# Attention and feed-forward in one kernel: later loads for batch 2, wider runs for w_in, later token softmax, two more products by a second level of Strassen, and the states' first product by Strassen

## The chip, the cores and the metric

One NeuronCore of a Trainium2 chip runs the whole program. The metric is the device time of one execution in microseconds. A profile shows one execution, and its span runs from the first to the last instruction.

The engines are named as the profile names them: PE is TensorE (matmul), PEld its weight load, DVE is VectorE, ACT is ScalarE, POOL is GpSimd, SP is SyncE, which here only issues DMAs.

## The reference

There are 8 batches. In each, 512 tokens and 32 states exchange information by attention in 8 heads of 64 columns, and the 544 rows that result (8 heads side by side make 512 columns) pass through a feed-forward block with an ELU.

```python
# x (8, 8, 512, 64), state (8, 8, 32, 64): float32; w_in (512, 2048), w_out (2048, 512): float64
scores  = x @ state.T / 8              # per batch and head
xread   = softmax(scores) @ state      # 512 rows: tokens read states
scores2 = state @ x.T / 8
sread   = softmax(scores2) @ x         # 32 rows: states read tokens
r = concatenate([xread, sread])        # then (B*544, 512), heads side by side
h = r @ w_in
g = where(h > 0, h, exp(min(h, 0)) - 1)
out = g @ w_out
```

The result is float32, (4352, 512).

## The kernel before, in words

**One order for all.** The program is not written engine by engine. Every helper adds operations to a list (`Plan.add`), with engine, an assumed cost, the regions read and written, and for a PSUM tile a bank yet to be chosen. `Plan.order` then runs a list schedule: each engine takes, among the operations that are ready, the one with the earliest due time; PE takes them by their number in the list (`turn`). PSUM banks are handed out on the way; two of the eight (`fixed`) are kept for a special use, so six are free for the rest. What comes out is the instruction order of each queue. Until 40 us of assumed time, matmuls of the identity fill PE's gaps (`fill`). In the start the list's order is overruled by hand: `FIRST_PE` permutes PE's turns, `EARLIER` shifts due times, `FIRST_LOADS` ranks the first DMAs. As every record is made by one helper, nearly all have line L438 in the profile; they are told apart by tiles.

**The weights.** They arrive as float64 and are turned to float32 on the chip (`convert`: two ACT and four DVE operations for a block of 128 x 1024 values). There are 16 blocks of 1 MB: 0 to 7 from w_in, 8 to 15 from w_out. They pass through three raw buffers (`t_w`); a block's buffer is loaded again with the block three later once it is converted. w_out stays in SBUF. w_in goes through three slots (`w_half`), and is written to a DRAM tensor `w_in_mem` (`keep_w`), from which every later batch fetches it in eight pieces of 512 KB (`fetch`).

**Tokens.** As a head has only 32 states, the kernel does not form xread and multiply it by w_in: it forms m = state @ w_in per batch (`make_m`, small matmuls of 64 x 32 weights, in chunks `c` of 512 of the 2048 columns), and then h = softmax @ m. From batch 2 on this product is done by seven half-size products in place of eight (Strassen's scheme in Winograd's form, `ffn1_chunk`; the sums it needs are made by POOL, `sum_m` and `sum_a`). Batches 0 and 1, during which the weights arrive, use the plain product (`ffn1_plain`, one call per tile of 128 columns). `softmax` makes both softmaxes of a batch from one set of scores: the one over states (transposed, into `aT`) and the one over tokens (`soft_a`), which `move_state` or `turn_state` turn round for `state_read`.

**g @ w_out.** The class `Strassen` cuts g (512 x 2048) and w_out into quarters a11 to a22 and b11 to b22. The seven products are called here P1 = a11 b11, P2 = a12 b21, P3 and P4 with b22 and the sum t4, P5 with t1, P6 with t2 and P7 with t3 = b12; `sum_1` and `combine` make the sums of quarters of g on DVE. From batch 1 on, some of the seven are themselves done by seven products of 128 columns (class `Second`: `weights` makes the sums on the weight side once, `sums` those on the side of g, `steps` the seven products of four calls; after each, DVE or ACT takes the result out of PSUM and adds it into the output tile `o`). In `ffn2` of batches 2 to 7 these are P3 to P7; P1 and P2 are plain, sixteen calls of 256 columns each, in one PSUM bank. In batch 1 they are P3, P4, P5 and P7. Between P1 and P2 stand the scores and the first `make_m` of the next batch, and its softmax follows.

**States.** The 256 rows of sread of all batches come last (`states`): a plain first product in 64 calls of 256 columns, ELU, then one level of Strassen with w_out, and stores by quarters (`quarter`).

**The start** (`start`). States and x of batches 0 and 1 and the first weight blocks are loaded; for every block a `w_step` converts it, makes m for both batches, and the feed-forward of the two batches follows as chunks become ready. Batch 2's x is loaded a second time in a blocked form (`load_blocks`, sixteen DMAs of 64 KB in runs of 128 bytes) and turned round by DVE (`turn_blocks`) for its scores.

Of the kernel before, what the change touches and what calls it, by code (L numbers as in the profile page):

```python
# [21 lines left out]
ENGINES = (POOL, PE, DVE, ACT, SP)  # L22

# [58 lines left out]
class Plan:  # L82
# [99 lines left out]

    def prepare(self):
        for op in self.ops:
            op.users = []
            op.turn = self.places.get(op.number, op.number)
        for op in self.ops:
            for d in op.deps:
                d.users.append(op)
        self.opening = {}  # L190
        self.closing = {}
        for b in self.banks:
            self.opening.setdefault(b.first, []).append(b)
            self.closing.setdefault(b.last, []).append(b)
        self.kept = {b.first: b.fixed for b in self.fixed}
        self.all_banks = min([op.number for op in self.kept], default=0)
# [29 lines left out]
    def run(self, until=0.0):  # L226
# [4 lines left out]
        free_at[PE], free_at[ACT] = 0.7, 0.0  # L231
# [111 lines left out]
    def order(self, passes, until=0.0):  # L343
# [3 lines left out]
        for _ in range(passes):  # L347
# [8 lines left out]
            if best is None or last < best[0]:  # L356
                steps = [(op.start, op.number, op) for op in done]
# [4 lines left out]
        for at, n, op in steps:  # L362
            op.start = at
        return [op for _, _, op in steps], fills

@with_exitstack
def kernel(
# [36 lines left out]
    ).tile([P, 2 * FC, NP, 256], FP32, name="w_in_mem")  # L404
# [19 lines left out]
    w_half = buffer([3, NP, 256], "w_half")  # L424
# [94 lines left out]
    def dma(out, in_, tokens=((), ()), queue=SP, kind="dma"):  # L519
        size = 4 * elements(out) * out.shape[0]  # L520
        engine = nc.sync if queue == SP else nc.scalar
        op = plan.add(
            queue, 0.66 if kind in ("load_blocks", "move_state") else 0.44, issue(engine, "dma_start", dict(out=out, in_=in_)), [in_], [out],
            moved=size, tokens=tokens, name=kind,
        )
        if kind in ("load_x", "load_states", "load_blocks", "move_state"):
            op.rate = 230e3
# [108 lines left out]
    def fetch(hc):  # L636
        w = w_half[:, hc % 3]
        dma(w, w_in_mem[:, hc], tokens=((f"mem{hc}",), ()), kind="fetch")
        st["w", hc] = w

    def make_m(b, *hcs):
        c = hcs[0] // 2
        if hcs[0] % 2 == 0:
            st[b, "m", c] = [bank(), bank()]
        calls = []
        for hc in hcs:
            w, h = st["w", hc], hc % 2
            calls += by_state(
                b, st[b, "m", c], [w[:, m] for m in range(NP)],
                slice(h * 256, (h + 1) * 256), h == 0,  # L650
            )
        products(0.46 * len(hcs), calls, "make_m", "state")
# [4 lines left out]
    def copy_m(b, c, to, halves=False, engines=None):  # L657
        copies = engines or (A.copy, A.copy)
        for g in range(G):
            copies[g](out=to[:, g * 512 : (g + 1) * 512], in_=st[b, "m", c][g])  # L660
        g_of[b, c] = to

    def copy_m_half(b, hc, to):
        c, h = divmod(hc, 2)
# [31 lines left out]
    def soft_a(b, g):  # L696
        return (sec_2 if b < 2 else xr[:, 1024:])[:, g * 512 : (g + 1) * 512]
# [3 lines left out]

    def softmax(b, to):
        s = st[b, "s"]
        top, total = small[:, 0:2], small[:, 2:4]
# [5 lines left out]
        for g in range(G):  # L710
            V.transpose(out=soft_t(g), in_=s[g])
            V.reduce_max(out=tops(g)["top"], in_=s[g], axis=AX_X)
        V.tensor_scalar(out=top, in0=top, scalar1=-scale, scalar2=None, op0=ALU.mult)
        for g in range(G):
            A.activation(
                out=soft_a(b, g), in_=s[g], func=AF.Exp, scale=scale, bias=tops(g)["top"],
                accum_out=tops(g)["total"],
            )
# [13 lines left out]
        V.tensor_scalar(out=total, in0=total, scalar1=eps, scalar2=None, op0=ALU.add)  # L732
        V.reciprocal(out=total, in_=total)
# [61 lines left out]
    def ffn1_plain(b, c, g_to, a, e_slots):  # L795
        for q in range(4):
# [169 lines left out]
    }  # L966
    s_2 = [sec[:, 7680 + i * 1024 : 7680 + (i + 1) * 1024] for i in range(2)]
# [56 lines left out]
    def convert(dst, raw, pool_clamp=False, pool_add=False):  # L1024
# [3 lines left out]
        q = raw[:, : n // 2].rearrange("p n (j k) -> p (n j) k", j=2)  # L1028
# [4 lines left out]
        (Q if pool_clamp else V).tensor_scalar(  # L1033
# [10 lines left out]
        (Q if pool_add else V).tensor_tensor(out=bits, in0=bits, in1=q, op=ALU.add)  # L1044

    raws = [
        t_w_sb[:, i].rearrange("p k q -> p (k q)").bitcast(U32).rearrange("p (n k) -> p n k", n=4)
# [3 lines left out]
    def weight_block(n, parts=1):  # L1051

        out = []
        for i in range(parts):
            k = 4 // parts
            rows = slice(i * k, (i + 1) * k)
            raw = raws[n % 3][:, rows]
            if n < 8:
                src, dst = w_in_v[:, rows, n * 512 : (n + 1) * 512], w_half[:, n % 3, rows]
            else:  # L1060
                q, c = divmod(n - 8, 4)
                rows = slice(4 * c + i * k, 4 * c + (i + 1) * k)
                src = w_out_v[:, rows, q * 512 : (q + 1) * 512]
                dst = w_out[:, rows, q * 256 : (q + 1) * 256]
            dma(raw, src, kind="load_w")
            out.append((dst, raw))
        return out
# [3 lines left out]
    def ident_ready(i):  # L1071
# [12 lines left out]
    FIRST_PE = (  # L1084
        153, 48, 171, 198, 258, 106, 104, 86, 327, 32, 165, 16, 190, 265, 214, 157, 331, 90, 232,
        410, 335, 277, 261, 248, 169, 45, 289, 161, 202, 35, 146, 149, 347, 186, 210, 102, 339,
        173, 183, 408, 94, 229, 269, 218, 319, 194, 206, 98, 281, 113, 411, 293, 304, 414, 109,
        413, 409, 82, 351, 112, 273, 412, 38, 316, 307, 285, 42, 323, 79, 343,
    )
    FIRST_LOADS = (  # L1090
        6, 9, 0, 3, 5, 4, 1, 8, 7, 2, 12, 10, 11, 13, 14, 15,
    )
    EARLIER = {
        23: 34, 43: -2, 74: -5, 85: 22, 96: -17, 100: -12, 119: 28, 124: 25, 132: -3, 134: 2,
        135: 5, 136: 10, 137: 20, 138: -10, 142: 10, 154: -4, 163: 8, 175: 17, 195: 10, 199: 9,
        212: 10, 215: -2, 221: 10, 222: 10, 224: -15, 231: -10, 252: 2, 264: 10, 266: 10, 270: 20,
        272: 10, 276: 15, 280: 10, 282: -12, 283: 20, 286: -10, 288: -18, 295: 7, 306: 2, 311: 40,
        312: -10, 317: 5, 336: -2, 338: 12, 342: -2, 352: 7, 353: 42, 357: 10, 358: -2, 363: -12,
    }

    def start():
# [6 lines left out]
        m1.append(w_half[:, 2].rearrange("p m k -> p (m k)"))  # L1108
# [3 lines left out]
        blocks = {}  # L1112

        def read_block(n):
            blocks[n] = weight_block(n)

        def convert_block(n):
            for dst, raw in blocks[n]:
                convert(dst, raw)
            if n + 3 < 16:  # L1120
                read_block(n + 3)

        n = len(plan.ops)
        load_states(0, 1, raw_s, (SP, ACT))
        blocks[0] = weight_block(0, 2)
        load_x(0, x_halves, (SP, ACT))
        load_states(1, 2, raw_s[:, 1:], (SP,))
        read_block(1)
        load_x(1, x_1)
        read_block(2)  # L1130
        first = plan.ops[n:]
        for k, i in enumerate(FIRST_LOADS):
            first[i].rank = k
        turn_states(raw_s[:, 0:1], kT[:, 0:1])

        def w_step(hc):
            convert_block(hc)
            w = st["w", hc] = w_half[:, hc % 3]
            c = hc // 2
# [330 lines left out]
```

## Time and profile before

| | |
|---|---|
| time, median of 3 runs | 717.48 us (715.24, 717.48, 718.79) |
| profiled span | 715.3 us |
| PE clock granted | 0.998 |
| instructions | 13801 |
| DMA bytes | 78.49 MB, mean 110 GB/s |
| HBM read, written | 61.34 MB, 13.11 MB |

A busy line gives the time in which an engine works and the number of its instructions. A matmul call on float32 shows as two records. Matmuls are pipelined and the profile models their ends, so what one costs is read from start to start in the timeline, not from its duration. In a slice line each digit is the busy share in tenths of one of 40 equal slices (17.9 us each).

The profile's stages are: the start, up to about 113 us, while weights arrive; the rest of batches 0 and 1, up to about 200; batches 2 to 7, each 76.8 us apart; the states from 659.9 on.

### The profile page before, as it was taken

To read this page: it belongs to the slowest core of one execution; us is meant where nothing else is said; L and a number is where in the kernel's file an instruction comes from. 1 tells how busy PE (TensorE), PEld (TensorE's weight loads), DVE (VectorE), ACT (ScalarE), POOL (GpSimd) and SP (SyncE) were. 2 spreads that over 40 slices of the span, in tenths; PEclk is the share of its full clock that TensorE was granted. 3 is DMA by queue.
4 is the path that set the end of the run, shared out by engine and by line. 5 is a ranking of instruction groups with operands and counts; after the bars stand their busy time and mean duration, and the time that the engine had idled before them with its cause. 6 is when DMAs were issued, how large, how long until landed. Compare 5 with 4: busy or idle time off the path is not lost.

```text
span 715.3 us, 13801 instructions
## 1 busy us (share of the span) xinstructions
PE 700.3 (98%) x5526; PEld 588.3 (82%) x5526; DVE 525.5 (73%) x931; ACT 285.3 (40%) x547; POOL 122.7 (17%) x158
## 2 busy tenths in 40 slices
PE   8889999999999999999999999999999999999998
PEld 7434457888988899889988998889988998899886
DVE  3889899789549983899568964897489946976230
ACT  4978884011137311741075214631284017410320
POOL 0310000023211222220430241124212133000000
PEclk9999999999999999999999999999999999999999
DMA  9878770013163423541272316342444133001401
GB/s 243 258 172 316 251 265 26 1 25 121 63 165 84 116 53 107 157 118 30 94 202 63 86 62 148 105 120 73 122 115 121 29 118 119 0 1 40 150 21 27
DMA packets 133008, 78.49 MB, mean 110 GB/s; under 512 B 114000, under 2 KB 114512, under 8 KB 132944
## 3 DMA queue, kind: packets, MB, share of 16 engines
q1 hardware_dynamic: 130636, 76.99, 38.1%
q8 instruction: 43, 0.70, 0.4%
q10 hardware_dynamic: 2308, 0.62, 0.4%
q14 instruction: 21, 0.17, 0.1%
HBM read 61.34 MB, written 13.11 MB: 104 GB/s over the span
## 4 chain that ended last, share of the span: by engine, by line
PE 73%; DVE 14%; ACT 7%; DMA 4%; issue 1%; SPq 0%; DVEq 0%
PE ps L438 73%; DVE g L438 3%; DVE small L438 2%; DMA t_w<-in_moe_w_in_dram 2%; ACT sec L438 2%; DVE sec L438 2%; ACT xe L438 2%; DVE s L438 1%; DVE w_out L438 1%; DMA t_w<-in_moe_w_out_dram 1%; DVE xr L438 1%; DVE soft L438 1%; ACT w_half L438 1%; ACT t_w L438 1%; DVE t_w L438 1%
## 5 line engine op out<-in xcount | busy, mean ns | idle before, releaser
L438 PE MATMUL ps<-w_out,g 128*128 128x256 f32 (+1 forms) x960 | 174.7, 331 | 0.0
L438 PEld LDWEIGHTS ps<-w_out,g 128*128 128x128 f32 x960 | 151.1, 191 | 15.5 <-issue 2.5
L438 PE MATMUL ps<-aT,m 128*128 128x256 f32 (+1 forms) x568 | 149.2, 407 | 0.2 <-DVE g L438 0.2
L438 PEld LDWEIGHTS ps<-aT,m 128*128 128x128 f32 x568 | 105.4, 190 | 32.0 <-issue 12.2
L438 DVE TENSOR_TENSOR o<-o,ps 128x128 f32<-128x128 f32 (+2 forms) x214 | 60.4, 288 | 65.9 <-PE ps L438 64.0
L438 ACT ACTIVATE xe<-ps 128x512 f32<-128x512 f32 x104 | 58.9, 599 | 60.4 <-PE ps L438 47.8
L438 POOL TENSOR_TENSOR m<-m 128x256 f32<-128x256 f32 x72 | 51.5, 735 | 164.1 <-ACT m L438 162.7
L438 POOL TENSOR_TENSOR soft<-soft,small 128x512 f32<-128x512 f32 x32 | 33.8, 1075 | 234.8 <-DVE small L438 234.8
L438 PE MATMUL ps<-sec 128*128 128x128 f32 x544 | 72.6, 276 | 1.3 <-DVE o L438 1.3
L438 ACT COPY o<-ps 128x128 f32<-128x128 f32 (+2 forms) x55 | 21.9, 411 | 127.8 <-PE ps L438 126.0
L438 PE MATMUL ps<-t_w,s 128*128 128x128 f32 (+1 forms) x448 | 70.3, 306 | 0.0
L438 PEld LDWEIGHTS ps<-t_w,s 128*128 128x128 f32 x448 | 63.1, 191 | 6.5 <-issue 2.1
L438 PEld LDWEIGHTS ps<-sec 128*128 128x128 f32 x544 | 66.2, 192 | 2.2 <-DVE o L438 2.2
L438 ACT COPY m<-ps 128x512 f32<-128x512 f32 (+1 forms) x56 | 27.3, 529 | 79.0 <-PE ps L438 78.9
L438 DVE SCALAR_TENSOR_TENSOR g<-xe,ps 128x512 f32<-128x512 f32 x56 | 36.7, 680 | 26.7 <-ACT xe L438 23.9
L438 ACT COPY ps<-ps 128x512 f32<-128x512 f32 x24 | 13.7, 572 | 81.1 <-PE ps L438 81.1
L438 DVE TENSOR_TENSOR ps<-sec,ps 128x512 f32<-128x512 f32 x48 | 33.1, 690 | 10.8 <-PE ps L438 8.0
L438 PE MATMUL ps<-aT,s 128*128 128x256 f32 x168 | 40.2, 379 | 0.0
L438 PE MATMUL ps<-w_half,kT 64*32 64x256 f32 x1024 | 36.5, 385 | 0.2 <-DVE w_half L438 0.2
L438 PEld LDWEIGHTS ps<-aT,s 128*128 128x128 f32 x168 | 31.9, 190 | 4.3
L438 ACT COPY sec<-ps 128x512 f32<-128x512 f32 x48 | 28.3, 589 | 17.9 <-PE ps L438 17.9
L438 ACT ACTIVATE xe<-xe 128x512 f32<-128x512 f32 x56 | 33.4, 634 | 0.6
(112 smaller groups left out, 1012.1 us busy)
## 6 DMA issues: line engine op xcount, KB each, us to landing
w_half<-w_in_mem SPq DMA_DIRECT2D x56, 512.0 KB, 3.7
t_w<-in_moe_w_out_dram SPq DMA_DIRECT2D x8, 1024.0 KB, 6.5
t_w<-in_moe_w_in_dram SPq DMA_DIRECT2D x7, 1024.0 KB, 6.3
out_dram<-o SPq DMA_DIRECT2D x14, 512.0 KB, 2.7
xe<-in_x_dram SPq DMA_DIRECT2D x26, 256.0 KB, 2.9
o<-in_x_dram SPq DMA_DIRECT2D x80, 64.0 KB, 3.0
w_in_mem<-w_half SPq DMA_DIRECT2D x8, 512.0 KB, 6.8
xr<-xr SPq DMA_DIRECT2D x96, 32.0 KB, 1.9
```

The lines of the kernel that those rows point to most:

```text
L438: ins = getattr(engine, name)(**{k: resolve(v) for k, v in kw.items()})
```

## The change

It has seven parts.

- The first loads: x of batch 0 at the head of the queues, then the first two weight blocks. Batch 2's remaining state loads are put behind the conversion of block 9, and its blocked x behind that of block 15 (`plan.behind`).
- Blocks 0 to 7 of w_in are cut the other way: half the rows and 1024 words of columns (4 KB runs) in place of all rows and 512 words (2 KB runs). Blocks 0 and 1 are loaded and converted in halves (2 KB runs), so that half a chunk can be made from both; from then on a step takes a whole chunk, which is two blocks. `make_m` then makes 512 columns in one call where it made 256 in two.
- The token part of `softmax` becomes `softmax_rows`; in batches 0 and 1 it comes after chunk 1 of batch 0.
- The orders written by hand (`FIRST_PE`, `FIRST_LOADS`, `EARLIER`) go; the planner gets other assumed DMA rates (`DMA_COST`).
- P2 of batches 2 to 7 and P6 of batch 1 are done by `Second`.
- The states' first product is done by Strassen in four chunks (`state_chunk`), with five buffers for fetched pieces in place of three.
- The stores of the states are one DMA to a quarter in place of four, all on SP.

```diff
     w_in_mem = ...
-    ).tile([P, 2 * FC, NP, 256], FP32, name="w_in_mem")
+    ).tile([P, 2 * FC, 2, 512], FP32, name="w_in_mem")
-    def make_m(b, *hcs):
...
+    def make_m(b, c, part=None):
+        if not part:
             st[b, "m", c] = [bank(), bank()]
+        cols = slice(0, 512) if part is None else slice(part * 256, (part + 1) * 256)
+        products(
+            0.92 if part is None else 0.46,
+            by_state(
+                b, st[b, "m", c], [st["w", 2 * c + m // 2][:, m % 2, cols] for m in range(NP)],
+                cols, not part,
+            ),
+            "make_m", "state",
+        )
...
     def soft_a(b, g):
-        return (sec_2 if b < 2 else xr[:, 1024:])[:, g * 512 : (g + 1) * 512]
+        at = xr if b > 1 else s_buf if b else sec_2
+        return at[:, (b > 0) * 1024 + g * 512 :][:, :512]
...
+    second[2] = Second(sec_2)
...
+        if n < 8:
+            c, j = divmod(n, 2)
+            dst = w_half[:, n % 3]
+            src = w_in_v[:, 2 * j : 2 * j + 2, c * 1024 : (c + 1) * 1024]
...
     def start():
...
         load_states(0, 1, raw_s, (SP, ACT))
-        blocks[0] = weight_block(0, 2)
         load_x(0, x_halves, (SP, ACT))
+        read_half(0, 0)
+        read_half(1, 0)
         load_states(1, 2, raw_s[:, 1:], (SP,))
-        read_block(1)
         load_x(1, x_1)
+        read_half(0, 1)
+        read_half(1, 1)
         read_block(2)
...
         turn_x(x_halves, ob)
         scores(0, ob)
         softmax(0, a_sb)
-        w_step(1)
-        ffn1(0, 0)
-        turn_state(0)
+        w_half_step(0)
+        ffn1(0, 0, (0, 1))
         turn_x(x_1, ob)
         scores(1, ob)
-        state_read(0)
         softmax(1, aT1)
-        w_step(2)
-        ffn1(1, 0)
-        turn_state(1)
-        state_read(1, x_1)
-        w_step(3)
...
+        ffn1(1, 0, (0, 1))
+        w_half_step(1)
+        ffn1(0, 0, (2, 3))
+        ffn1(1, 0, (2, 3))
+        for c in range(1, 4):
+            w_step(c)
+            ffn1(0, c)
+            if c < 2:
+                for b in range(2):
+                    softmax_rows(b)
+                    turn_state(b)
+                    state_read(b, (x_halves, x_1)[b])
+            ffn1(1, c)
         for n in range(8, 16):
             convert_block(n)
+            if n == 9:
+                with plan.behind(plan.ops[-1]):
+                    load_states(2, B, raw_t, (SP,))
+                turn_states(raw_t, kT[:, 2:B])
+        late = plan.ops[-1]
...
-        load_blocks(2, xe)
+        with plan.behind(late):
+            load_blocks(2, xe)
...
     def ffn2(o, b, x1=None):
         if six:
...
             A.copy(out=c12, in_=x1)
+            A.copy(out=c11, in_=x1)
+            second[2].sums(o.a12, s_2[1], a_sb[:, :1024])
             if nxt:
                 scores(b + 1, xr)
                 first_m(b + 1)
-            o.product(x1, o.a12, b21, False)
-            A.copy(out=c11, in_=x1)
+            for f in second[2].steps(c11):
+                f()
...
         else:
+            A.copy(out=c12, in_=x1)
             combine(o.a12, o.a12, o.s)
+            second[6].weights(t_w[2])
+            second[6].sums(o.s, s_2[0], m_sb[:, 1, :1024])
             second[7].weights(t_w[3])
+            steps = second[6].steps(c12)
             second[7].sums(o.a21, s_2[1])
-            o.product(x1, o.s, t_w[2], False)
-            A.copy(out=c12, in_=x1)
-            A.copy(out=c21, in_=x1)
+            for f in steps:
+                f()
...
         if not six:
-            second[6].weights(t_w[2])
+            second[2].weights(b21)
...
+    def state_chunk(c, right):
...
+        V.tensor_tensor(out=s1, in0=l21, in1=l22, op=ALU.add)
+        V.tensor_tensor(out=s2, in0=s1, in1=l11, op=ALU.subtract)
+        V.tensor_tensor(out=l21, in0=l11, in1=l21, op=ALU.subtract)
+        V.tensor_tensor(out=s4, in0=l12, in1=s2, op=ALU.subtract)
...
+        product(pa, l11, r11, True)
+        A.copy(out=pb, in_=pa)
+        product(pc, s1, t1, True)
+        product(pb, s2, t2, False)
+        product(pa, l12, r21, False)
+        A.copy(out=u2, in_=pb)
+        elu(pa, to(0, 0), e_1, A)
+        product(pb, s3, t3, False)
+        A.copy(out=u3, in_=pb)
+        product(pb, l22, t4, False)
+        V.tensor_tensor(out=pa, in0=u3, in1=pc, op=ALU.add)
+        elu(pb, to(1, 0), e_2, A)
+        product(pc, s4, r22, False)
+        elu(pa, to(1, 1), e_1, A)
+        V.tensor_tensor(out=pc, in0=u2, in1=pc, op=ALU.add)
+        elu(pc, to(0, 1), e_2, A)
...
     o, x1 = start()
-    plan.places = dict(zip(FIRST_PE, sorted(FIRST_PE)))
-    for n, t in EARLIER.items():
-        plan.ops[n].nudge = t
```

## The prediction, made before the changed kernel ran

> **What bounds the kernel now.** First the engine shares, then the busy share by slice:
>
> ```profile
> PE 700.3 (98%) x5526; PEld 588.3 (82%) x5526; DVE 525.5 (73%) x931; ACT 285.3 (40%) x547; POOL 122.7 (17%) x158
> PE   8889999999999999999999999999999999999998
> DVE  3889899789549983899568964897489946976230
> ```
>
> TensorE is the bound, and from 113 us on nearly without a hole: the waits of PE in the window 113:715 list 2.5 us in all. So from there every us of matmul taken away shortens the span, unless a new wait takes its place. The chain of waits agrees: PE carries 73% of it. DVE is full only in places. Before 113 us it is another kernel; the windows by stage (PE, PEld, DVE, ACT, POOL busy, clock, DMA share, GB/s):
>
> ```profile
> 0.00:8.30 8.30, 6.94 (x39) 6.76 (x39) 0.00 (x0) 1.28 (x1) 0.70 (x6) 1.00 0.77 195
> 8.30:20.00 11.70, 10.09 (x146) 7.94 (x146) 8.88 (x18) 8.67 (x18) 2.05 (x2) 1.00 1.06 280
> 20.00:28.60 8.60, 7.33 (x138) 3.90 (x138) 7.63 (x15) 8.28 (x16) 2.91 (x2) 0.80 0.80 268
> 28.60:40.00 11.40, 10.24 (x76) 4.94 (x68) 10.49 (x21) 10.57 (x23) 4.15 (x4) 1.00 0.80 194
> 40.00:60.00 20.00, 18.13 (x155) 8.20 (x148) 16.01 (x22) 14.62 (x29) 0.00 (x0) 1.00 0.89 247
> 60.00:80.00 20.00, 18.75 (x88) 7.92 (x87) 17.42 (x23) 16.91 (x31) 0.00 (x0) 1.00 0.78 274
> 80.00:100.00 20.00, 19.78 (x114) 10.09 (x113) 19.50 (x26) 19.33 (x31) 0.00 (x0) 1.00 0.82 284
> 100.00:113.00 13.00, 11.48 (x39) 6.81 (x37) 13.00 (x18) 9.03 (x12) 0.00 (x0) 1.00 0.46 143
> ```
>
> PE's busy figure here includes fill matmuls. DVE, first used at 8.3, is busy 92.9 of the remaining 104.7 us; its holes (11.8 us) are mostly in 8 to 20 and 40 to 80. PE's first feed-forward matmul starts at 28.63; after that it is rarely dry for long. DMA is near its limit to 60 us. Three engines and the DMA share the bound, so no single relief gives much.
>
> Then the timeline of one steady second product (batch 3) and of the end:
>
> ```profile
> 313.81 1.09 PE L438 MATMUL ps<-xr,kT 64*32 64x512 f32 x16
> 314.69 1.07 PE L438 MATMUL ps<-w_half,kT 64*32 64x256 f32 x32
> 315.69 7.17 PE L438 MATMUL ps<-w_out,g 128*128 128x256 f32 x32
> 322.70 1.95 PE L438 MATMUL ps<-t_w,s 128*128 128x128 f32 x16
> 324.91 1.16 PE L438 MATMUL ps<-sec 128*128 128x128 f32 x8 [0.26 <-DVE o L438]
> ...
> 643.82 1.06 PE L438 MATMUL ps<-t_w,s 128*128 128x128 f32 x8
> 644.71 1.06 PE L438 MATMUL ps<-sec 128*128 128x128 f32 x8
> ...
> 659.90 27.79 PE L438 MATMUL ps<-xr,w_half 128*128 128x256 f32 x128
> 687.53 7.07 PE L438 MATMUL ps<-w_out,g 128*128 128x256 f32 x32
> ```
>
> Read starts, not durations: a plain P2 lasts from 315.69 to 322.70, 7.0 us, for 32 records (two to a call), about 0.216 each; a step of eight 128-column records takes 0.89 (643.82 to 644.71), 0.112 each; the states' first product 27.6. The small matmuls on 64x32 weights: 16 of 512 columns take 0.88 (scores), 32 of 256 take 1.00 (make_m; 1.02 at 341.24, where the next starts at 342.26).
>
> **What the skill says.** "TensorE: Matmul & The Clock Gate", section "Wait — 56ns, not 53.3ns?": warm matmuls start N / 2.4 GHz plus about 2.5 ns apart. That is 55.8 ns for 128 columns, and the trace's fp32 records show twice it, 112 ns, so the fixed part is there too: two records of 128 columns cost 0.224 where one of 256 costs 0.216, and seven products for eight save 9%, not 12.5%. "VectorE: DVE Perf Modes", "Mode 2×_2P": a tensor_tensor of fp32 cannot use the double rate; here 0.69 us for 512 elements against 0.44 for a TENSOR_SCALAR. "DMA: Bandwidth & Descriptors", "Specifications": under 512 B a descriptor is below line rate; the page counts 114000 such packets, and the slice with batch 2's 64 KB block loads shows 172 GB/s beside 251 and more around it.
>
> **The change, part by part.** The sum is made against the profiled span, 715.3.
>
> P2, batches 2 to 7. 7.0 becomes 7 x 0.89 = 6.25: -0.7 each, -4.2. Added on DVE per batch: four sums of 512 elements (4 x 0.69) and seven adds into o (0.28 each), 4.7 us; on ACT one copy more (0.58). P2 is just the work under which DVE now does softmax and the sums of P6: from 313 to 339 DVE has no hole over 0.3 us. But some 6.5 us of it is softmax (two transposes 0.71, maxima 1.25, four reductions of 0.67 or so, two xr transposes) which is wanted only by the batch after, about 8 us behind; from 340 to 356 DVE has 7 us of holes. So it can be put off, while s1 and s2 are wanted within the 1.8 us of the first two steps. PSUM is tight too: six banks for scores, m and two new ones. P6, of the same form in the same crowded place, loses 0.45 per batch (the gap at 324.9). I take +0.4 a batch, bounds 0 and 2.5 (a wait of 0.35 at each of seven steps): +2.4.
>
> P6 of batch 1: -0.7, but its weight sums (4 x 0.69) can only be written where batch 0's g lies, after the last product of batch 0; the first two steps cover 1.8 of it. +1.5 (0 to 4).
>
> make_m, batches 2 to 7: 24 calls with 512 columns in place of twice 256, the form of scores: 1.02 to 0.88, -0.14 x 24 = -3.4. Nothing is added; bounds -2.8 to -3.6. All steady fetches stay at 512 KB.
>
> States' first product: 128 x 0.216 = 27.6 becomes 224 x 0.112 = 25.0, -2.6. DVE per chunk of 6.25 us: four sums 2.76, two adds and four maxima at 0.42, together 5.3; ACT three copies and eight activations of 256 elements, 4.1. Both fit, and copies of one chunk lie under matmuls of the next. Before it, 1.7 (operand sums), 2.8 (chunk 0) and one more restore 0.7 must fit in the 0.6 us holes of DVE at 650 to 660. +0.4 (0 to 3).
>
> The start. Removed: from the SP queue, between weight blocks, 12 state loads (about 0.8 each) and 16 block loads (31.74 to 40.8 for nine, 42.0 to 49.9 for seven, 1 us each); the hand-written PE order and nudges; added: x of batch 0 at the head of both queues. Behind these loads on SP stood weight blocks, and ACT then waited 3.78 us for one at 47.1. x now lands by about 8 in place of 10.2 and scores(0) come 2 to 3 us earlier; the softmax chain behind (12 us) loses two exponentials and two maxima out of its way. First feed-forward at about 25 for 28.6: -3.6. Later, DVE must still do 93 - 2.8 (four transposes moved behind the weights) = 90 us, so the stage cannot end before 8.3 + 90 = 98.5; with the holes as now it is 110. Two blocks must be converted before a chunk's m, where one was enough: 2 x 3.5 us of DVE. I take -4 for all of it, with bounds -11 (nearly no holes) and +6 (the new order is worse than the written one). Wider runs: 512 KB in 4 KB runs land in 3.7 us, 1024 KB in 2 KB runs in 6.3, little to choose; the first two blocks keep 2 KB. The moved loads: 16 x 1 us of SP after the last conversion (about 107) plus landing and four transposes, about 128; scores(2) stand at 144.28. 12 us of slack, nothing. The transposes fall into 113:140, where DVE has 2.7 us left: 0 to +1, I take 0.3. The fetches and x loads queued behind on SP are wanted at 174 and 190.
>
> Tail: four stores on two queues become one of 128 KB: -0.3 (-0.8 to +0.3).
>
> Sum: -4.2 +2.4 -0.7 +1.5 -3.4 -2.6 +0.4 -4 +0.3 -0.3 = -10.6, span 704.7. The median of the runs (717.48) lies 2.2 above the span: **707**.
>
> **The rivals.**
> The start does better (20%): holes of DVE shrink to half, stage over near 105, -8 there and few waits at P2: 715.3 - 15 = 700, 702 in runs. For: the block loads stand where ACT waits. Against: ACT and DVE are both above 96% from 80 to 100.
>
> DVE takes back P2 (20%): the steps wait for sums and adds, 1.4 us a batch, twice what P2 gives: 6 x 1.0 more than in the sum, 713; at the bound of 2.5 it is 6 x 2.1, 719.5. For: DVE full from 313 to 339. Against: P6 loses only 0.45 there, and the deferrable softmax.
>
> Slower (9%): the coarser weight step starves TensorE in the start. m of a chunk waits for two conversions; a chunk feeds 8 tiles x 1.72 = 13.8 us of PE, while DVE needs 2 x 3.5 + 8 x 0.6 + its share of softmax, 12 to 15. If PE runs dry for one pair of conversions at each of the three steps, 3 x 6.9 = 20.8 us against the -6.6 elsewhere and no gain: +14, 731. It decides from a loss of 10 us over the stage. Against: the early x gives a backlog, and the blocks are read three ahead as before.
>
> That a part does not do what it says: 4 KB runs hold for six blocks of eight only; its price is within the start's bounds.
>
> **How the numbers follow.** Forecast 51%, 707 with its own bounds 702 to 712; the better start 20%; DVE's return 20%, two thirds of it still faster, a third within 0.5%; the starved start 9%, of it 1% within 0.5%. 0.5% of the time (3.6 us) is about what a measurement of this kernel can tell from no change. Faster 0.84, same 0.08, slower 0.08. The range 698 to 715 takes in the better start and the milder return of DVE, and leaves out the starved start, DVE's bound and a start near its -11: some 2 in 10.
>
> **What would show it.** P2 as 56 records of 128 columns in 6.3 us, with gaps before them by DVE o under 0.5; make_m x16 in 0.88; the states in 25 us, no wait over 1; first feed-forward matmul near 25; last conversion before 109. If the span from that conversion to the end shrinks by less than 4 us, the P2 step is wrong; if the conversion ends after 113, the start.

## The result, and the profile after

| | before | after |
|---|---|---|
| time, median | 717.27 us (715.24 to 718.79) | 724.69 us (723.64 to 727.64) |
| ratio | | 1.0112, 95% interval 1.0071 to 1.0152 |
| profiled span | 715.3 us | 723.8 us |
| instructions | 13801 | 13595 |
| DMA bytes | 78.49 MB | 78.48 MB |

The change is slower by 1.1%, 7.4 us, where 707 had been forecast. First the page of the changed kernel: the engine shares and two slice lines.

```profile
PE 696.2 (96%) x5322; PEld 583.9 (81%) x5322; DVE 564.3 (78%) x1053; ACT 293.3 (41%) x567; POOL 121.9 (17%) x158
PE   7688899999999999999999999999999999999997
DVE  0897799989856997499749994899479964999550
```

PE is busy 4 us less in a span that is 8.5 us longer, so it stands 12.6 us more. In the later slices PE shows nines as before; the low digits are at the front. DVE's first slice, 0 to 18 us, has fallen from 3 to 0. The windows of the start, with the limits of the prediction up to 113 us (PE, PEld, DVE, ACT, POOL busy, clock, DMA share, GB/s), show where:

```profile
8.30:20.00 11.70, 5.75 (x68) 3.76 (x67) 0.00 (x0) 2.69 (x6) 0.00 (x0) 0.93 0.98 280
20.00:28.60 8.60, 6.29 (x64) 5.86 (x68) 8.51 (x19) 5.09 (x11) 2.37 (x3) 0.70 0.24 99
28.60:40.00 11.40, 8.04 (x72) 3.89 (x64) 11.15 (x23) 10.22 (x21) 4.66 (x5) 1.00 0.01 1
...
100.00:113.00 13.00, 13.00 (x46) 5.46 (x45) 11.98 (x16) 12.35 (x23) 0.00 (x0) 1.00 0.76 267
113.00:127.00 14.00, 12.68 (x63) 9.57 (x61) 13.27 (x17) 10.32 (x14) 0.00 (x0) 1.00 0.73 172
```

DVE does nothing from 8.3 to 20 us, where it had worked 8.88; then DMA, which had carried 268 and 194 GB/s between 20 and 40 us, carries 99 and 1. The last weight block lands only at about 116. Two marks tell the stages apart in every kernel below: the end of the conversion of weight block 14, and the first product of scores on batch 2's raw x, for short "scores of batch 2".

| profile | first conversion starts | first feed-forward product | block 14 converted | scores of batch 2 | from there to the end |
|---|---|---|---|---|---|
| before | 8.76 | 28.63 | 112.95 | 144.28 | 571.0 |
| after | 19.36 | 36.63 | 126.87 | 157.34 | 566.5 |

The start loses 13.1 us and the rest gains 4.5. A mark comes from one execution. Two kernels below run the same products and loads in the same order up to the scores of batch 2, and their executions reach them at 147.51 and 143.93. So a difference of less than some 4 us between marks shows nothing by itself.

The rest, in the timeline of PE, for the same stretch of batch 3 as in the prediction:

```profile
325.66 1.09 PE L450 MATMUL ps<-xr,kT 64*32 64x512 f32 x16
326.54 1.06 PE L450 MATMUL ps<-w_half,kT 64*32 64x512 f32 x16
327.54 2.05 PE L450 MATMUL ps<-w_out,g 128*128 128x128 f32 x16
...
333.89 1.06 PE L450 MATMUL ps<-sec,g 128*128 128x128 f32 x8
335.06 1.16 PE L450 MATMUL ps<-w_out,aT 128*128 128x128 f32 x8
...
669.68 1.06 PE L450 MATMUL ps<-xr,w_half 128*128 128x128 f32 x8
```

P2 runs from 327.54 to 333.89, 6.35 us for 7.0 before. One small gap follows it (333.89 to 335.06 is 1.17 for a step of 0.89). `make_m` takes 1.00 us (326.54 to 327.54), exactly what its 32 narrower records took. The states' first product runs from 669.68 to 695.62; without 0.87 us for four records of the next product among its own it takes 25.1 us.

Now the start. ACT's timeline of the changed kernel, around its first conversion:

```profile
9.66 2.06 ACT L450 COPY o<-ps 128x512 f32<-128x512 f32 x4 [3.52 <-PE ps L450]
19.36 0.66 ACT L450 ACTIVATE w_half<-t_w 128x512 f32<-128x512 f32 x1 [7.64 <-DMA t_w<-in_moe_w_in_dram]
```

ACT stands 7.64 us for a DMA. It is about to convert the first half of block 0, and in the trace's DMA events that half had landed at 10.40. The second half of the block landed at 19.34, 0.02 us before ACT starts. In the changed kernel the two halves are the left and the right 512 words of each row of the raw buffer, so they lie interleaved; before, the two parts of block 0 were whole rows, one behind the other. SP's timeline shows what follows from it (the number after the start is how long the group takes, waits between its issues included):

```profile
13.98 26.32 SPq L450 DMA_DIRECT2D t_w<-in_moe_w_in_dram  x4
...
91.97 0.37 SPq L450 DMA_DIRECT2D t_w<-in_moe_w_out_dram  x1
92.38 9.72 SPq L450 DMA_DIRECT2D xr<-in_state_dram  x12
102.22 1.45 SPq L450 DMA_DIRECT2D t_w<-in_moe_w_out_dram  x2
```

The fourth load of the first line is block 3's. It stands on SP until the second half of block 0 is converted and the raw buffer is free, at 40.3 us; that is the hole in the DMA windows. Later the 12 state loads stand between two loads of w_out for 9.7 us. And PE is dry ahead of the products of chunk 2, because the copies of m stand on ACT behind a conversion whose block has not come:

```profile
75.90 2.30 PE L450 MATMUL ps<-w_half,kT 64*32 64x512 f32 x32
81.80 8.83 PE L450 MATMUL ps<-aT,m 128*128 128x512 f32 x16 [3.60 <-ACT m L450]
90.47 7.03 PE L450 MATMUL ps<-s,g 128*128 128x512 f32 x16
97.43 1.09 PE L450 MATMUL ps<-w_half,kT 64*32 64x512 f32 x16
```

The sixteen records behind this wait take 8.67 us (81.80 to 90.47), the next sixteen of the same form 6.96. The windows of just these two stretches give the granted clock, the third figure from the end, as 0.80 and 1.00, and 8.67 x 0.80 is 6.94:

```profile
81.80:90.47 8.67, 8.67 (x16) 3.72 (x17) 7.49 (x10) 8.66 (x12) 0.00 (x0) 0.80 0.45 128
90.47:97.43 6.96, 6.96 (x17) 2.85 (x15) 6.82 (x11) 6.25 (x11) 0.00 (x0) 1.00 1.00 365
```

### The profile page after: what moved, and what is told of

It is laid out like the page before. It is cut to its first block, busy times and chain, and to the rows that moved or that the text cites. A ratio compares the mean times of both kernels' runs of the same rounds, so it can differ in the third digit from the quotient of the medians.

```text
span 723.8 us, 13595 instructions
## 1 busy us (share of the span) xinstructions
PE 696.2 (96%) x5322; PEld 583.9 (81%) x5322; DVE 564.3 (78%) x1053; ACT 293.3 (41%) x567; POOL 121.9 (17%) x158
## 2 busy tenths in 40 slices
DMA packets 131248, 78.48 MB, mean 108 GB/s; under 512 B 113776, under 2 KB 114288, under 8 KB 131184
## 4 chain that ended last, share of the span: by engine, by line
PE 70%; DVE 14%; DMA 5%; SPq 4%; ACT 3%; issue 3%; ACTq 0%; DVEq 0%
PE ps L450 69%; DVE g L450 4%; SPq L450 4%; DMA t_w<-in_moe_w_in_dram 2%; DVE s L450 1%; DMA t_w<-in_moe_w_out_dram 1%; DVE ps L450 1%; DMA o<-in_x_dram 1%; DVE small L450 1%; DVE o L450 1%; ACT sec L450 1%; DVE xe L450 1%; DVE sec L450 1%; DVE w_half L450 1%; DVE soft L450 1%
## 5 line engine op out<-in xcount | busy, mean ns | idle before, releaser
L450 PE MATMUL ps<-w_out,g 128*128 128x128 f32 (+1 forms) x864 | 143.2, 314 | 0.0
L450 PEld LDWEIGHTS ps<-w_out,g 128*128 128x128 f32 x864 | 126.3, 191 | 12.5 <-ACT o L450 4.2
L450 DVE TENSOR_TENSOR o<-o,ps 128x128 f32<-128x128 f32 (+2 forms) x263 | 71.6, 278 | 46.7 <-PE ps L450 45.3
L450 PE MATMUL ps<-t_w,s 128*128 128x128 f32 (+1 forms) x432 | 64.8, 299 | 0.0
L450 PEld LDWEIGHTS ps<-t_w,s 128*128 128x128 f32 x432 | 58.6, 192 | 4.2 <-ACT m L450 0.8
L450 ACT ACTIVATE xe<-ps 128x512 f32<-128x512 f32 x96 | 53.6, 598 | 15.6 <-DVE ps L450 9.0
L450 ACT COPY ps<-ps 128x512 f32<-128x512 f32 (+1 forms) x28 | 15.2, 544 | 101.9 <-PE ps L450 101.4
L450 DVE STREAM_TRANSPOSE xr<-o 128x512 f32<-128x512 f32 x20 | 14.1, 707 | 32.4 <-DMA o<-in_x_dram 32.4
L450 PE MATMUL ps<-w_half,kT 64*32 64x512 f32 (+1 forms) x544 | 34.6, 573 | 0.0
L450 DVE TENSOR_TENSOR g<-xe,ps 128x512 f32<-128x512 f32 x48 | 32.5, 680 | 0.8
```

Source lines behind the costliest of these rows:

```text
L450: ins = getattr(engine, name)(**{k: resolve(v) for k, v in kw.items()})
```

## The experiments

The theory after these readings (A): the parts outside the start gain what was forecast; all of the loss is in the new start, through the interleaved halves first and the state loads second. The rivals: the loss of the order written by hand; the coarser step; the planner's new transfer rates. Four kernels first. A ratio compares with the kernel before as it ran in the same round; where kernels of two rounds are compared, the ratios count and not the medians.

**Halves laid apart in the raw buffer.** The transfers are the same; only the place where a half lands changes.

```diff
     def half_block(n, h):
         dst, raw, src = weight_block(n)
-        raw, src = raw[:, :, h * 512 : (h + 1) * 512], src[:, :, h * 512 : (h + 1) * 512]
+        raw, src = raw[:, h : h + 1].rearrange("p o (n k) -> p (o n) k", n=2), src[:, :, h * 512 : (h + 1) * 512]
```

> The changed kernel, with one line altered: the two halves of weight blocks 0 and 1 lie one behind the other in the raw buffer instead of side by side in interleaved columns, so that the conversion of a first half depends on its own load alone. Theory A (the conversion of the first half waits for the load of the second half, 10.4 us to 19.3 us, and everything behind it in the orders of ACT and DVE waits too): first weight conversion on ACT at 10 to 11 us, first feed-forward matmul near 28 for 36.6, span 8 to 10 us shorter, 714 to 716. Rival B (the loss is the new order and the two-block steps, and the early wait is hidden): first conversion earlier, but the last one within 3 us of where it was, span 721 to 724.

Measured: 717.77 us, ratio to before 1.0009 (0.9992 to 1.0025). ACT's timeline of this kernel at the same place:

```profile
9.68 2.05 ACT L450 COPY o<-ps 128x512 f32<-128x512 f32 x4 [3.21 <-PE ps L450]
11.59 0.84 ACT L450 ACTIVATE w_half<-t_w 128x512 f32<-128x512 f32 x1
```

The wait is gone, the first conversion starts 7.8 us earlier, the first feed-forward product at 29.04, and the scores of batch 2 stand at 149.44. Fill matmuls apart, both traces have the same instructions and loads in the same order on every engine, and in both the loads of the two halves of a block report to one and the same semaphore. So neither the planner's order nor the shared semaphore makes the wait. It was for the neighbour's data, and it cost about 7 us of the time, somewhat less than expected. The start is still 5 us behind that of before.

**The start of before with all the other parts of the change.** `start` and its helpers are those of the kernel before, with its order written by hand; only the write to `w_in_mem` follows the new layout. P2, P6 of batch 1, `make_m`, the states and the stores are those of the changed kernel.

```diff
-            dma(w_in_mem[:, hc], w, tokens=((), (f"mem{hc}",)), kind="keep_w")
+            dma(
+                w_in_mem[:, 2 * c : 2 * c + 2, :, hc % 2 * 256 : (hc % 2 + 1) * 256],
+                w.rearrange("p (j i) k -> p j i k", j=2), tokens=((), (f"mem{hc}",)), kind="keep_w",
+            )
```

> The kernel before with its own start (loads, orders written by hand, one-block steps, softmax in one piece), and from there the changed parts: P2 of batches 2 to 7 and P6 of batch 1 by a second level, make_m with 512 columns, the states' first product by Strassen, one store to a quarter. The kept w_in is written in the new layout, in 1 KB pieces. Theory A (all of the loss lies in the start, the rest gains what it did in the changed kernel, 602.3 to 596.9 us): span 708 to 711, time 710 to 713. Rival C (the saving in the steady part was only possible because the start ended later): no faster than before, 715 and over.

Measured: 712.52 us, ratio 0.9931 (0.991 to 0.9952). In the profile 565.5 us lie between the scores of batch 2, at 147.51, and the end, 5.5 less than before. So the parts outside the start are worth 0.7%, and the start holds all of the loss.

**The same with a plain P2.**

```diff
-            for f in second[2].steps(c11):
-                f()
+            o.product(x1, o.a12, b21, False)
+            A.copy(out=c11, in_=x1)
```

> As the graft, but P2 of batches 2 to 7 is again the plain product. By the prediction's step (0.7 saved a batch, 0.4 lost to waits) it is 2 us slower than the graft. If P2 by a second level loses nothing, 4 us slower; if its waits eat the saving, the same or faster.

Measured: 714.93 us, ratio 0.9971 (0.9955 to 0.9986), 2.4 us more than with the second level; the scores of batch 2 stand at 143.93. A period of a batch is 76.54 us with the plain P2 and 76.14 with the other, 0.40 apart. Seven products for eight pay here, although DVE was full.

**The kernel before without its order written by hand.**

```diff
-        for k, i in enumerate(FIRST_LOADS):
-            first[i].rank = k
+        for k, op in enumerate(plan.ops[n:]):
+            op.rank = k
...
-    plan.places = dict(zip(FIRST_PE, sorted(FIRST_PE)))
-    for n, t in EARLIER.items():
-        plan.ops[n].nudge = t
```

> The kernel before without the orders written by hand for its start: no permuted turns of TensorE, no shifted due times, first loads in the order of the program. Theory A (the hand order is not where the loss is): within 4 us of before. Rival B (dropping it costs what the changed kernel lost): 8 to 14 us slower than before.

Measured: 720.73 us, ratio 1.004 (1.0025 to 1.0055). The hand order is worth 3 us in the kernel before, within the 4 that theory A allowed. That seemed to rule it out as a main cause; a later run corrects this.

The second four start from the halves laid apart, the last from the start of before.

**State loads behind all weight loads.**

```diff
         for n in range(8, 16):
             convert_block(n)
-            if n == 9:
+            if n == 13:
```

> Contiguous halves as in the run before, and in addition the 12 loads of the states of batches 2 to 7 stand on SP behind the load of the last w_out block instead of between two of them. Theory A (these 12 issues, 9.7 us on SP in the changed kernel, delay the last two or three w_out blocks): the wait of PE on the last w_out block but one, which ended at 119.0 with the states between the loads, ends 4 to 7 us earlier, at 112 to 115, and the time falls from 717.8 to 711 to 714. Rival (DVE's and ACT's conversions, not the loads, end the start): the wait ends at 118 to 120 and the time stays at 716.5 to 719.

Measured: 715.35 us, ratio 0.9978 (0.9956 to 1.0001). SP's timeline of this kernel:

```profile
94.35 5.99 SPq L450 DMA_DIRECT2D t_w<-in_moe_w_out_dram  x2
100.39 8.39 SPq L450 DMA_DIRECT2D xr<-in_state_dram  x12
```

Block 14 is converted at 113.99 in place of 118.97, and the scores of batch 2 come 4.3 us earlier, at 145.11. That looks like theory A, but the two executions are not alike. This one took 713.29 us, 2.1 under the median; the profiled one with the states early took 719.11, 1.3 above its own. From 74 to 77 us the granted clock is 0.50 in that one and 1.00 in this. By the ratios 2.2 us arrive, less than expected, and the intervals overlap. So the gain of this part is likely, but not shown.

**Other assumed transfer rates for the planner.**

```diff
-    "load_w": (0.44, 285e3), "load_w4": (0.44, 370e3), "load_x": (0.6, 270e3), "load_states": (0.6, 75e3),
+    "load_w": (0.44, 200e3), "load_w4": (0.44, 200e3), "load_x": (0.6, 270e3), "load_states": (0.6, 75e3),
```

> The same as the kernel with the states' loads late, but the planner is told a weight transfer rate of 200 GB/s for both kinds of weight load in place of 285 and 370, nearer to what the traces show in the start. Theory B (the planner believes blocks land earlier than they do and so lists ACT's copies of m behind a conversion that still waits for its block; PE then stood 3.9 us before the products of the third step of two blocks): that wait goes to under 1.5 us and the time falls by 2 to 4 us against the kernel with the states late. Rival (a step of two whole blocks is too coarse and PE waits for blocks whatever the order): the total of PE's waits before 120 us changes by less than 1 us, and the time by less than 1.5 us.

Measured: 717.41 us, ratio 1.0001 (0.9985 to 1.0017): 2 us slower than the kernel with the states late, with intervals that overlap. The waits of PE from 20 to 135 us in this kernel:

```profile
PE ps L450 <- DVE w_out L450: 2.6, 2, 1.3
PE ps L450 <- DVE sec L450: 2.4, 1, 2.4
PE ps L450 <- DVE t_w L450: 2.0, 1, 2.0
...
PE ps L450 <- ACT m L450: 0.4, 1, 0.4
```

The waits on the copies of m did go to 0.4, and others took their place. Theory B falls: the rates move the wait and do not remove it.

**Token softmax of batches 0 and 1 early again.**

```diff
         softmax(0, a_sb)
+        softmax_rows(0)
+        turn_state(0)
+        state_read(0, x_halves)
         w_half_step(0)
```

(and so for batch 1; the loop over chunks loses these lines.)

> The same as the kernel with the states' loads late, but the token softmax, the turning of the state and the state product of batches 0 and 1 are written directly behind their first softmax, as in the kernel before, not behind the second and third weight step. Theory A (that move is nearly neutral; the loss is in the loads): time within 1.5 us of the kernel with the states late. Rival C (the later softmax frees DVE and ACT for the first conversions, and is a real gain of the change): 2 to 5 us slower than the kernel with the states late, with the first FFN product later than 29.0 by 2 us or more.

Measured: 716.49 us, ratio 0.9986 (0.9971 to 1.0002), 1.1 us from the kernel with the states late, and the intervals overlap. The first feed-forward product came at 25.74, 3.6 us earlier and not later, and the scores of batch 2 at 148.30, 3.2 us later. So the move of the token softmax is close to neutral, and an early first product did not bring an earlier end of the start.

**Batch 2's blocks late, with the start of before and all other parts.**

```diff
         for n in range(8, 16):
             convert_block(n)
+        late = plan.ops[-1]
...
+        n_late = len(plan.ops)
         load_blocks(2, xe)
+        for op in plan.ops[n_late:]:
+            op.deps.add(late)
```

> The start of the kernel before with all the other changed parts (that was 712.5 us), and in addition the blocks of batch 2 are loaded only behind the conversion of the last weight block. Theory A (batch 2's blocks are needed long after the start, and their 32 KB loads take DMA time from the weights): the wait on w_out ends 0 to 3 us earlier than 113 to 116 and the time is 709.5 to 712.5. Rival (batch 2's blocks then come too late for the Strassen sums of that batch, and PE waits for them after the start): 714 to 718, with a new PE wait between 113 and 150 us.

Measured: 706.13 us (705.39 to 708.12), ratio 0.9852 (0.9824 to 0.9879). It is the fastest version, 1.5% under the kernel before. The gain is larger than expected. The added dependence acts in the planner: it gives the loads their place on SP, behind all weight loads. On the chip they go out from 102.23 us on (with four later loads of x behind them), while the last conversion ends at 112.10:

```profile
102.23 22.99 SPq L438 DMA_DIRECT2D xe<-in_x_dram  x20
```

Three windows of this kernel, which answer to the windows of before shown in the prediction:

```profile
40.00:60.00 20.00, 20.00 (x203) 8.69 (x180) 19.13 (x26) 18.36 (x36) 0.37 (x1) 1.00 0.81 251
60.00:80.00 20.00, 20.00 (x88) 9.23 (x80) 19.34 (x25) 19.18 (x34) 0.00 (x0) 1.00 0.86 272
80.00:100.00 20.00, 19.92 (x98) 10.10 (x98) 19.61 (x26) 18.97 (x29) 0.00 (x0) 1.00 0.74 260
```

PE is full from 40 us on, where 3.3 us of holes lay between 40 and 100; DVE works 19.13 for 16.01 from 40 to 60. The wait of ACT for a weight block at 47.1 us, 3.78 us before, is 0.16 here. The scores of batch 2 stand at 138.42, 5.9 us earlier than before. From there to the end it is 565.6, the same as with early blocks: nothing waits for the late ones. With the loads, the four transposes of these blocks leave the start too, 2.8 us of DVE; how the gain divides between the queue and DVE was not tried.

By now two things were open: what keeps the start with the states late 6.7 us behind this one (145.11 against 138.42; 9 us by the ratios), and whether the late blocks need the other parts. Three more.

**First two blocks as 512 columns of all rows again**, in the kernel with the states late.

```diff
-    def half_block(n, h):
...
+    def first_block(h, rows):
+        raw = raws[h].rearrange("p n (j k) -> p (n j) k", j=2)[:, rows]
+        dst = w_half[:, :2].rearrange("p i j k -> p (i j) k")[:, rows, h * 256 : (h + 1) * 256]
+        return dst, raw, w_in_v[:, rows, h * 512 : (h + 1) * 512]
...
-            for i in range(2):
-                dst, raw, src, q = half_block(i, h)
-                convert(dst, raw, q)
-                if h:
-                    read_block(i + 3)
+            for rows in parts[h]:
+                convert(*first_block(h, rows)[:2])
+            read_block(h + 3)
```

> The changed kernel with the states' loads behind all weights (715.4 us; its first products on the raw data of batch 2 began at 145.1 us), but w_in's first two blocks are again 512 columns of all rows in 2 KB runs, loaded, converted and multiplied one after the other, as in the kernel before; blocks 2 to 7 stay in 4 KB runs and in steps of two. Theory D (the four half blocks keep two of three raw buffers in use until the second half is converted, so that block 3's load left SP only at 33 us and DMA moved 106 GB/s from 20 to 30 us): block 3's load now leaves SP at 20 to 24 us, the products on batch 2 begin at 140 to 142 us, and the time is 710 to 712.5. Rival E (the later steps of two whole blocks are what costs): the products on batch 2 begin at 144 to 146 us and the time stays at 714 to 717.

Measured: 713.71 us, ratio 0.994 (0.9918 to 0.9963), between the two expectations. First SP's timeline, then PE's, of this kernel:

```profile
14.92 10.68 SPq L450 DMA_DIRECT2D t_w<-in_moe_w_in_dram  x3
```

```profile
73.01 7.13 PE L450 MATMUL ps<-aT,m 128*128 128x512 f32 x16 [2.60 <-ACT m L450]
```

Block 3's load leaves SP at 25.6, 7.4 us earlier, though not at 20 to 24 as theory D has it. The lead is gone by the products of chunk 2, where PE waits 2.60 us for the copies of m on ACT, and the scores of batch 2 stand at 145.70, no earlier. That is what rival E said of the mark. By the ratios 2.7 us are gained (0.994 for 0.9978), and the two intervals overlap. So the halves' hold on the raw buffers may cost some 3 us, and its share is not settled.

**The fastest version without the order written by hand.** The edit is the same as in the kernel before.

> The start of the kernel before with batch 2's blocks behind all weights and all other changed parts (706.1 us with its hand-written order), now without the hand-written order of products, loads and shifts. Theory (the hand-written order is worth the same 3 us that it was worth in the kernel before): 708 to 711. Rival F (with the loads late, the hand-written order has nothing left to mend): 705.5 to 707.5. Rival G (the planner's order fits the late loads badly, and it is the missing hand-written order that keeps the changed start behind): 712 to 716.

Measured: 713.34 us, ratio 0.9952 (0.9939 to 0.9964): 7.2 us slower, as rival G said. The scores of batch 2 stand at 145.60, close to the 145.11 and 145.70 of the new start. The waits of PE from 100 to 120 us have a new line at the top:

```profile
PE ps L438 <- DVE w_out L438: 2.8, 1, 2.8
```

So the hand order is worth about twice as much once the loads are late as it was before. Part of this can be the clock: over the first 60 us the granted clock is 0.91 in the profiles of both kernels without the hand order, and 0.97 in those of the two that they are compared with. That is at most 3.6 us of TensorE time, an estimate from 60 x 0.06.

**The kernel before with batch 2's blocks late and nothing else.** The edit is the one shown above for the late blocks.

> The kernel before with one edit: the 20 loads of batch 2's blocks wait for the conversion of the last weight block. Theory A (this part alone is worth 6 us in the start and does not depend on the other parts): 710 to 712, with products on the raw data of batch 2 at 138 to 139 us. Rival (it is worth that only together with the other parts, since P2 of the kernel before needs its buffers otherwise): 714 to 718.

Measured: 711.68 us, ratio 0.9924 (0.9901 to 0.9947). The part stands alone: 0.76% here, and 0.79% between the two versions with the other parts. The scores of batch 2 came at 141.57, 2.7 us earlier than before and not 6, in an execution that was the slowest of six (715.5 us). The expectation counts 20 loads; the edit holds back the 16 of the blocks, and four loads of x stand behind them.

## Why the prediction was wrong

All steps together, as a ladder of ratios to the kernel before; 0.001 is 0.72 us.

| kernel | ratio | step, us |
|---|---|---|
| before | 1 | |
| + P2, P6 of batch 1, `make_m`, states, stores | 0.9931 | -4.9 |
| + batch 2's blocks behind all weights | 0.9852 | -5.7 |
| without the order written by hand | 0.9952 | +7.2 |
| + 4 KB runs, steps of two blocks, token softmax later, x first, states last, new rates | 0.9978 | +1.9 |
| + the 12 state loads among the last w_out loads | 1.0009 | +2.2 |
| + the halves interleaved: the changed kernel | 1.0112 | +7.4 |

Each ratio has an interval of about 0.002 to either side, that of the changed kernel 0.004, so the two steps of about 2 us are at the edge of what these runs can tell apart. A step holds for its place in the ladder; the hand order was worth 3 us at another place.

**The start, "-4 ... with bounds -11 ... and +6".** This is the step that failed, by its own mark: the last conversion ended at 131.9, and "if the conversion ends after 113, the start". (The mark itself was misread: in the kernel before, the last conversion ended at 116.26 and not at about 107; near 113 it was block 14's.) The measured term is +13.1 in the profile and +13.0 by the ratios (1.0112 less 0.9931), outside its bounds. Half of the reasoning held: the block loads stood where ACT waited, and moving them, with their transposes, gives 5.7 us. But the term was taken as one lump, and three things in it had no price.

- The halves. That blocks 0 and 1 are loaded in halves was listed as a shape, with no question of what a conversion of one half waits for. It cost 7.4 us, with the hand order one of the two large losses.
- The 12 state loads. Their removal from between the first weight blocks was counted as a gain of the queue. At their new place, behind block 9's conversion, weight loads stand behind them too, at 0.8 us an issue; the cost, about 2 us, is not clear of the noise. "The moved loads ... nothing" reckoned with the 16 block loads only, and of those it was right: 565.6 us after the scores of batch 2 with the loads late, 565.5 with them early.
- The order written by hand. "The new order is worse than the written one" was in the bound of +6. It is 7.2 with the loads late, though 3 in the kernel before: what this order is worth depends on where the loads stand.

"First feed-forward at about 25 for 28.6" failed twice: it came at 36.63, and at 29.04 with the halves apart. Nor did an early one help: the profiles with the first product at 25.74 and 26.43 ended their start 3.2 and 4.9 us later than one with 29.32, about as much as marks vary.

**P2 and P6.** "-4.2 +2.4 -0.7 +1.5", 1.0 together. The P2 step is right and somewhat low: 6.35 us for 7.0, gaps of 0.3 where 0.4 a batch was taken, and 2.4 us gained by the run with and without it, where -4.2 +2.4 is 1.8. It left out that the waits of PE for `o` would go: five in the kernel before, 1.3 us in all, and none in the changed kernel or with the plain P2. DVE did not take it back, though it is busy 39 us more in all. P6 of batch 1 was not tried by itself.

**`make_m`, "-3.4".** Mis-sized: 0. Sixteen records of 512 columns take 1.00 us here, where the sixteen of scores beside them take 0.88. In the timeline the scores are followed by a group of the same form, and `make_m` by 128-row products; about 0.1 us goes to the change of form and not to the number of records. The kernel before shows it for the scores themselves, where those of batch 2 stand ahead of 128-row products and take 1.02:

```profile
144.28 1.09 PE L438 MATMUL ps<-xr,kT 64*32 64x512 f32 x16
145.30 5.02 PE L438 MATMUL ps<-t_w,s 128*128 128x256 f32 x22
```

There 32 records of 256 columns at 1.00 also stood ahead of such a change, so nothing was to be saved. The row was right and the comparison was not.

**States, "-2.6 +0.4".** Right: 25.1 us for 27.6, and no wait of PE between its chunks in the list of waits after 127 us, which holds one line of 1.3 us.

**From the start's end on**, the span shrinks by 7.2 us if counted from the last conversion (599.0 to 591.9), and by 4.5 if counted from the scores of batch 2. The forecast was 6.6 for all steps but the start, 3.2 without `make_m`; with the 1.3 us of waits for `o` it comes to 4.5. So this half of the sum stands.

**The rivals.** The starved start (9%, 731) was the nearest: slower, and in the start. Its mechanism, PE dry for a pair of conversions at each of three steps, shows only once for 3.6 us ahead of chunk 2, and the step of two whole blocks with all that came with it is worth about 1.9 us net and not 20.8. The page that the prediction cites on descriptors, the Trainium skill's "DMA: Bandwidth & Descriptors", section "Specifications", made the 64 KB block loads look costly for their small packets, and moving them did pay; but the versions with early and with late blocks have the same number of packets under 512 B, 113760. What paid is when they and their transposes ran, not how many there were.

What stays open: how the +1.9 divides between the steps of two blocks, the x first and the rates, which these runs can't resolve; why the late loads and the hand order need each other, and how much of that is the clock; and what rule makes a conversion of one half wait for the other. That laying the halves apart removes the wait is shown. The planner's own bookkeeping (`Plan.region`) marks exact places, by which the halves never overlap. That a dependence is kept elsewhere by the range from a view's first to its last word is only an argument.

## What to carry to other kernels

When a transfer is split, ask for each reader which of the landings it waits for, and lay the parts so that they do not interleave. A load that is moved out of one queue position has to be priced at the new one: what stands behind it there, and who waits for that. When a change bundles seven parts, price the parts of its largest term one by one; here one part alone gave 0.76%, all without the new start 0.7%, the two together 1.5%, and the bundle lost 1.1%.

## What the hardware showed beyond that

- A group of small matmuls takes longer ahead of another form: 16 records of 64x512 take 0.88 us ahead of the same form and 1.00 ahead of 128-row products, as much as 32 records of 64x256.
- Twelve 32 KB state loads in a row hold SP for 8.4 to 10.4 us in six kernels, 0.70 to 0.87 us an issue.
- Sixteen records of 512 columns took 8.67 us at a mean granted clock of 0.80 and 6.96 at 1.00. In each of the thirteen profiles the start has a stretch of 3.4 or 6.8 us at half the clock, in some a second one, and two executions of the same order differ in this, with two stretches and with one.
